# A new hand-written order for a 24-unit kernel: the same operations in another sequence, some on another engine or queue, and fewer warming matmuls

## The chip, the cores and the metric

The kernel runs on one core of a Trainium2 chip. That core has five instruction streams: TensorE (PE in the profile, with its weight loads as PEld), VectorE (DVE), ScalarE (ACT), GpSimd (POOL) and SyncE (SP, which here only starts DMAs). Each stream executes in order, and an instruction that has to wait holds up all that is queued behind it on its own stream. The metric is the device time of one execution in microseconds (us); lower is better. Three executions of the kernel before took 167.09, 168.38 and 167.21 us, median 167.21.

## The reference

Two layers follow one another. The first is a recurrence over time with a decaying state, for 4 batches, 8 heads, 768 steps and 48 channels a head. The second is a two-matrix network with a softmax-weighted activation and a layer norm, over 3072 tokens, 384 model channels and 1024 hidden channels.

```python
for t in range(S):
    cur = einsum('bhd,bhe->bhde', u * k[t], v[t])
    y[t] = einsum('bhd,bhde->bhe', r[t], state + cur)
    state = w[t][..., None] * state + einsum('bhd,bhe->bhde', k[t], v[t])
x = y.transpose(0, 2, 1, 3).reshape(B * S, H * D)
h = x @ w_in
sm = exp(h - max(h)) / sum(exp(h - max(h)))
solu = h * sm
ln = (solu - mean(solu)) / sqrt(var(solu) + 1e-6) * g_ln
out = ln @ w_out
```

## The kernel before

**Units.** The 768 steps are cut into 6 chunks of 128, and with 4 batches this makes 24 units of 128 tokens with all 8 heads; unit i is chunk i // 4 of batch i % 4. A unit needs four inputs of 192 KB each (w, k, r, v). Within a chunk the recurrence becomes matrix work: cumulative sums of log w by two triangular matmuls (`cum`), exponentials of both (`ex`, ScalarE), k and r scaled by them (`kp`, VectorE), transposes of both (`krk`, `krr`) and one copy out of PSUM (`kr`), 8 score matmuls of 64 channels (`M`), a masked copy of the scores (`m`, by VectorE with the mask in the same instruction, or by ScalarE with `sel`, a mask by GpSimd, behind it), and the attention matmuls (`Y`). The bonus term with u is made on the side: p = k * r, q = p * u (GpSimd), its sum `dg` (VectorE), dv = v * dg (GpSimd). It is added to y by VectorE in `y`, or, where ScalarE copies y, by an identity matmul at the head of `Y` ("i" in place of "n"). `vb` rounds v to bf16. The state of a batch goes from chunk to chunk by `S` (matmuls), `et` (ScalarE) and `st` (VectorE).

**The second layer of a unit.** `X` transposes y and `xT` copies it out; `H` is 24 matmuls with w_in; `e` = exp (ScalarE), `he` = h * e (VectorE), `hq` = he squared (VectorE or ScalarE); `Oa` and `Ob` are 12 matmuls each (4 of 385 columns with w_out, 8 of one column for the sums). `sq`, `qm` and `lv` make the row's scale, `o` applies it (ScalarE or VectorE), `out` stores 192 KB. w_out is prepared once: multiplied by g (`gw`, 8 parts), its column mean taken by 8 matmuls into PSUM (`mn`), and the mean added to all 8 parts (`ce`, VectorE). `Oa` of unit 0 cannot start before the last `ce`. w_in is rounded by `wi` (3 parts). Unit 23's second layer is done in halves (`Ha`, `Hb` and their like). Units 20 to 23 get two of their transposes by DMA (`KD`, `XD`, on SyncE's queue).

**What sets the order.** Everything is one list of words, ORDER (lines 21 to 69). A word names a stage, a unit (or a part), and behind the dot an engine, a queue or a PSUM slot: "d", "a", "p" are VectorE, ScalarE and GpSimd; for loads and stores "s" or nothing, "a", "p" are the queues of SyncE, ScalarE and GpSimd; "b0", "s3" and their like are PSUM slots. The loop at lines 563 to 566 emits the stages in that sequence, and the class InOrder (line 74) ties every instruction to the one before it on its engine, so that the list is the program order of every stream. Nothing reorders it afterwards. (All of these instructions are recorded at line 88, the line inside InOrder, so the profile is read by tiles and not by lines.)

```python
    for word in ORDER.split():
        word, _, how = word.partition(".")
        name = word.rstrip("0123456789")
        stages[name](int(word[len(name):]), how)
```

**Rings.** Input tiles are rings of 7 units (NIO), the bf16 v and log w rings of 10, kp/kr/dv rings of 6, the rest 4. [...] `hot` runs are matmuls of 512 columns on a zero tile whose result nobody reads.

**The squares.** Line 470 holds the stage that the prediction turns on; on VectorE both operands are the same bf16 tile in SBUF:

```python
    def hidden_square(i, x, part=ALL):
        he, hq = he_t[i % NWK][:, part], hq_t[i % NWK][:, part]
        if x == "a":
            act.activation(out=hq, in_=he, func=SQUARE)
        else:
            (dve if x == "d" else pool).tensor_mul(out=hq, in0=he, in1=he)
```

Of the kernel before, what the change touches and what calls it, by code (L numbers as in the profile page):

```python
# [30 lines left out]
dv4 ce0 vb5.a krk6.s3 LK8.s H3.b1 et4 ce5 p5 e2 ce6 LR8.s ce2 p6 LV7.a krr6 ce4 Y4.is1 lw7 he2 e3 q5 LW9.s
Oa0.s2 vb6.p hq1.a LK9.s he3 M5.b0 q6 Ob0 y4.a LR9.s LV8.p m5.a kr6.d cum7.b1 Oa1.s1 hq2.d ex7 LW10.s sel5 st4
X4.s3 sq0 M6.b0 lw8 kp7 LK10.s Ob1 xT4.a p7 m6.a qm0 dg5 krk7.s0 LR10.s cum8.b1 hq3.d lv0 krr7 S5.s3 sq1 q7 dg6
ex8 LW11.s H4.b0 qm1 kr7.d o0.a dv5 kp8 LK11.s lv1 Oa2.s2 out0.p e4 o1.d LR11.s dv6 Y5.ns0 dg7 lw9 krk8.s1 y5.d
vb7.p et5 M7.b1 LW12.s Ob2 he4 sel6 m7.a LK12.s X5.s0 lw10 krr8 p8 st5 cum9.b1 vb8.a cum10.b0 xT5.d LR12.s sq2
ex9 kr8.d Oa3.s3 q8 ex10 kp9 LW13.s S6.s0 dv7 Ob3 hq4.a qm2 kp10 LV9.s p9 M8.b1 sq3 et6 lv2 krk9.s1 qm3 st6
H5.b0 p10 LK13.s lw11 m8.d lv3 p11 o2.a LR13.s krr9 dg8 e5 Y6.is0 q9 kr9.d LW14.s cum11.b1 krk10.s2 y6.a he5
S7.s1 out1.p ex11 LV10.s Oa4.s0 q10 lw12 kp11 o3.a krr10 out2 cum12.b0 sel7 et7 X6.s3 st7 ex12 M9.b1 kr10.d
LK14.s Ob4 q11 m9.a xT6.d kp12 krk11.s1 LR14.s out3.p Y7.ns2 lw13 M10.b1 sq4 y7.d vb9.p S8.s3 m10.a LW15.s dg9
dv8 krk12.s2 cum13.b0 LK15.s dg10 krr11 LV11.p ex13 qm4 H6.b1 hq5.d LR15.s kr11.d lv4 sel9 et8 o4.a kp13 krr12  # L40
Y8.ns1 LW16.s e6 p12 Oa5.s0 y8.d st8 kr12.a LK16.s X7.s1 p13 M11.b0 xT7.d S9.s3 dg11 lw14 LR16.s vb10.p Ob5 he6
m11.a dv9 S10.s2 et9 LW17.s LV12.p hq6.d cum14.b1 et10 sq5 H7.b0 ex14 qm5 st9 LK17.s q12 st10 lv5 kp14 krk13.s1
sel10 LR17.s e7 Y9.ns3 krr13 y9.d X8.s2 M12.b1 p14 o5.a LV14.s he7 Oa6.s3 kr13.a dv10 LW18.s krk14.s0 m12.d lw15
Ob6 LV13.p xT8.a LK18.s lw16 cum15.b0 hq7.d sq6 M13.b1 ex15 krr14 q13 qm6 LR18.s m13.d Y10.ns1 lv6 Oa7.s2 sel11
LV15.a kp15 kr14.a H8.b1 vb11.p o6.d dv11 y10.d cum16.b0 e8 LW19.s dg12 X9.s3 q14 Ob7 xT9.d ex16 he8 LK19.s
out4.p X10.s1 krk15.s0 Y11.ns3 sq7 xT10.a vb12.p krr15 LV16.s kp16 p15 M14.b1 kr15.a S11.s1 y11.d out5 H9.b0
vb13.p et11 m14.a qm7 st11 p16 dg13 LR19.s lv7 krk16.s0 hq8.d e9 H10.b1 LW20.s o7.d dv12 vb14.a he9 out6.p krr16
LK20.s e10 X11.s3 Oa8.s1 q15 LV17.s dg14 xT11.a kr16.d M15.b0 q16 lw17 Ob8 out7 m15.a he10 sel14 S12.s2 LR20.s
sq8 lw18 Y12.ns3 hq9.a dv13 Y13.ns0 y12.d cum17.b0 LW21.s H11.b1 hq10.d et12 ex17 vb15.p st12 LK21.s p17 qm8
y13.d LR21.s S13.s3 e11 kp17 Oa9.s2 dv14 lw19 dg15 X12.s0 q17 cum18.b0 et13 lv8 st13 Ob9 xT12.a he11 p18 o8.a  # L50
X13.s3 Y14.ns0 sq9 vb16.a out8 Oa10.s1 q18 ex18 y14.d LW22.s qm9 xT13.d LV18.s lv9 cum19.b1 p19 dg16 S14.s0
LK22.s ex19 kp18 krk17.s3 Ob10 dv15 kp19 LR22.s sel15 M16.b0 sq10 hq11.a krr17 m16.d H12.b1 LW23.s q19 et14 o9.a
kr17.d lw20 out9.p X14.s2 H13.b0 e12 dg17 LV19.p xT14.d qm10 he12 Oa11.s3 dv16 e13 krk18.s2 st14 vb17.p cum20.b1
lv10 he13 Ob11 dv17 ex20 p20 Y15.ns0 o10.a dg18 H14.b0 hq12.a kp20 q20 lw21 y15.d KD20 krk19.s1 LV20.p sq11 e14
krr18 qm11 Y16.ns0 kr18.d M17.b1 out10.p krr19 y16.d LK23.s m17.a S15.s2 hq13.d LV21.s Oa12.s0 lv11 kr19.d p21
vb18.a M18.b1 he14 et15 X15.s1 o11.a sel17 Ob12 vb19.a dg19 m18.a cum21.b0 q21 xT15.d S16.s3 st15 sq12 X16.s1
ex21 out11.p H15.b1 qm12 xT16.a p22 kp21 et16 lv12 S17.s2 e15 hq14.d KD21 Y17.ns1 H16.b0 st16 sel18 vb20.a he15
et17 lw22 LR23.s dv18 o12.a Oa13.s3 dg20 e16 LV22.p y17.d M19.b1 Ob13 he16 m19.a q22 X17.s1 Oa14.s0 sq13 out12.p
xT17.a qm13 hq15.d lv13 cum22.b0 dv19 o13.d H17.b1 ex22 dg21 out13.p dg22 sel19 Ob14 kp22 e17 Oa15.s1 st17 p23
KD22 lw23 he17 hq16.a Y18.ns3 q23 cum23.b0 Y19.ns2 y18.d ex23 M20.b1 dv20 y19.d Oa16.s3 sq14 m20.a kp23 vb21.p  # L60
X18.s2 vb22.p Ob15 qm14 xT18.d KD23 lv14 dv21 X19.s2 sq15 M21.b0 hq17.d H18.b1 m21.a LV23.s xT19.d sel20 o14.d
qm15 lv15 out14.p Ob16 e18 dv22 S18.s2 o15.a Oa17.s0 he18 sel21 sq16 out15 Y20.ns1 M22.b0 hq18.d M23.b1 m22.a
Ob17 y20.d qm16 m23.d XD20 lv16 Y21.ns1 sel22 H19.b0 o16.a dg23 sq17 et18 vb23.p y21.d dv23 S19.s3 st18 e19 XD21
Oa18.s1 et19 he19 Y22.ns2 Ob18 y22.d H20.b1 sq18 qm17 qm18 XD22 st19 lv17 hq19.d Y23.ns2 e20 H21.b0 out16 y23.d
lv18 XD23 he20 Oa19.s3 e21 hq20.d H22.b1 he21 Ob19 e22 o17.d Ha23.b0 out17 sq19 he22 Oa20.s2 ea23 o18.a qm19
Hb23 hq22.d hq21.a out18 Ob20 Oa21.s0 sq20 lv19 qm20 hea23 o19.a Oa22.s1 eb23 out19.p Ob21 lv20 heb23 hqa23.a
Ob22 hqb23.d sq21 qm21 o20.d lv21 Sa23.s3 sq22 out20.p qm22 o21.d Sb23 lv22 Mal23.s2 sq23 o22.a out21.p Mar23.s0
qm23 Mbl23 lv23 out22 Mbr23 ol23.a or23.d outl23.a outr23
"""

NIO, NLW, NKP, NWK = 7, 10, 6, 4
# [525 lines left out]
```

## Time and profile before

| | |
|---|---|
| median of three executions | 167.21 us |
| the profiled execution: time, span | 167.09 us, 165.4 us |
| mean granted clock of TensorE | 0.948 |
| PE busy | 138.8 us (84%) |
| DVE busy | 139.3 us (84%) |
| ACT busy | 119.3 us (72%) |
| POOL busy | 113.5 us (69%) |
| DMA moved | 28.51 MB, mean 172 GB/s |
| start of `mn` on PE; start of `Oa` of unit 0 | 34.27 us; 46.65 us |

The span runs from the first to the last instruction, and 1.7 us of the time lie outside it. The table of the page that cuts the span in 40 slices gives each engine's busy tenths, one digit for 4.1 us. The view by windows gives the same with numbers, and with the granted clock of TensorE in each window: at 0.50 a matmul takes twice its time while PE counts as busy all the same. A timeline row has start, duration, engine and operands, and in brackets the idle time of the engine ahead of it with what ended that.

### The profile page before, as it was taken

To read this page: it belongs to the slowest core of one execution; us is meant where nothing else is said; L and a number is where in the kernel's file an instruction comes from. 1 tells how busy PE (TensorE), PEld (TensorE's weight loads), DVE (VectorE), ACT (ScalarE), POOL (GpSimd) and SP (SyncE) were. 2 spreads that over 40 slices of the span, in tenths; PEclk is the share of its full clock that TensorE was granted. 3 is DMA by queue.
4 is the path that set the end of the run, shared out by engine and by line. 5 is a ranking of instruction groups with operands and counts; after the bars stand their busy time and mean duration, and the time that the engine had idled before them with its cause. 6 is when DMAs were issued, how large, how long until landed. Compare 5 with 4: busy or idle time off the path is not lost.

```text
span 165.4 us, 5234 instructions
## 1 busy us (share of the span) xinstructions
PE 138.8 (84%) x2128; PEld 108.5 (66%) x2128; DVE 139.3 (84%) x238; ACT 119.3 (72%) x245; POOL 113.5 (69%) x139
## 2 busy tenths in 40 slices
PE   6585548845999999904999999999997999999991
PEld 2133336733978787803686898688886778888771
DVE  7028949599999999999899998999989995979661
ACT  3456288791799899960397798988997798546782
POOL 5057697999009999999893569669999399510030
PEclk9999985898799999995699999999999999999999
DMA  5999999997999907999968619195486156213215
GB/s 114 272 235 307 360 325 304 206 255 160 237 237 175 211 4 184 222 224 228 203 167 163 146 55 188 46 192 153 79 231 149 57 115 156 78 33 90 99 50 190
DMA packets 98665, 28.51 MB, mean 172 GB/s; under 512 B 94953, under 2 KB 96882, under 8 KB 98642
## 3 DMA queue, kind: packets, MB, share of 16 engines
q1 hardware_dynamic: 87040, 19.57, 56.1%
q0 software_dynamic: 2080, 6.75, 11.5%
q10 hardware_dynamic: 9522, 1.87, 5.5%
q8 instruction: 16, 0.26, 0.7%
q14 instruction: 7, 0.06, 0.1%
HBM read 22.03 MB, written 4.72 MB: 162 GB/s over the span
## 4 chain that ended last, share of the span: by engine, by line
PE 53%; DVE 18%; issue 8%; SPq 7%; DMA 6%; ACT 5%; ACTq 0%; DVEq 0%
PE o_ps L88 18%; PE h_ps L88 17%; SPq L88 7%; DMA win_f<-in_moe_w_in_dram 5%; PE y_ps L88 4%; PE s_ps L88 3%; DVE w L88 3%; PE m_ps L88 3%; PE kr_ps L88 3%; DVE kp L88 3%; DVE he L88 3%; PE cum_ps L88 2%; DVE st L88 2%; DVE hq L88 2%; DMA kr_in<-in_r_dram 2%
## 5 line engine op out<-in xcount | busy, mean ns | idle before, releaser
L88 PE MATMUL o_ps<-w,he 128*128 128x385 bf16 (+2 forms) x208 | 47.3, 317 | 0.9 <-DVE st L88 0.8
L88 PE MATMUL h_ps<-xT,win_sb 128*128 128x128 bf16 x576 | 38.6, 226 | 0.4 <-DVE m L88 0.4
L88 PEld LDWEIGHTS <-win_sb 128*128 128x128 bf16 x576 | 35.4, 102 | 1.1 <-issue 0.4
L88 DVE TENSOR_TENSOR he<-h_ps,e 128x1024 bf16<-128x1024 f32 (+1 forms) x25 | 29.4, 1175 | 6.1 <-ACT e L88 5.7
L88 PE MATMUL o_ps<-inv_col,e 128*128 128x1 bf16 x192 | 31.2, 166 | 0.0
L88 DVE TENSOR_TENSOR kp<-cum_ps,kr_in 128x768 bf16<-128x768 f32 x24 | 22.7, 948 | 9.8 <-DMA kr_in<-in_r_dram 7.4
L88 PE MATMUL o_ps<-one_col,hq 128*128 128x1 bf16 x192 | 30.6, 163 | 0.0
L88 ACT ACTIVATE e<-h_ps 128x1024 bf16<-128x1024 f32 (+1 forms) x25 | 24.8, 990 | 7.2 <-PE h_ps L88 6.8
L88 POOL TENSOR_TENSOR p<-kr_in 128x384 bf16<-128x384 f32 x24 | 24.9, 1043 | 5.2 <-DMA kr_in<-in_r_dram 5.2
L88 PEld LDWEIGHTS <-hq 128*128 128x128 bf16 x192 | 18.6, 98 | 13.0 <-issue 1.0
L88 POOL TENSOR_TENSOR q<-p,u_bc 128x384 bf16<-128x384 bf16 x24 | 22.9, 952 | 5.3 <-ACT u_bc L88 1.6
L88 ACT ACTIVATE cum_ps<-cum_ps 128x768 f32<-128x768 f32 x24 | 19.2, 802 | 8.9 <-PE cum_ps L88 4.8
L88 POOL TENSOR_TENSOR dv<-vb,dg 128x384 bf16<-128x384 bf16 x24 | 20.4, 850 | 6.0 <-DVE dg L88 4.2
L88 POOL TENSOR_SCALAR_AFFINE_SELECT m<-m 128x1024 bf16<-128x1024 bf16 x15 | 17.0, 1132 | 10.4 <-ACT m L88 9.9
L88 ACT CAST m<-m_ps 128x1024 bf16<-128x1024 f32 x15 | 15.3, 1017 | 10.8 <-PE m_ps L88 10.4
L88 DVE TENSOR_TENSOR hq<-he 128x1024 bf16<-128x1024 bf16 (+1 forms) x16 | 20.9, 1308 | 0.1
L88 POOL DMA_DIRECT2D out_dram<-o x14 | 8.2, 584 | 18.5 <-ACT o L88 13.9
L88 PEld LDWEIGHTS <-he 128*128 128x128 bf16 x208 | 19.6, 96 | 1.5 <-DVE o L88 0.3
L88 PEld LDWEIGHTS <-kp 128*128 128x128 bf16 x240 | 15.7, 99 | 7.4 <-DVE kp L88 4.8
L88 PEld LDWEIGHTS <-e 128*128 128x128 bf16 x192 | 18.4, 97 | 1.2 <-issue 1.0
L88 PE MATMUL kr_ps<-ident,kp 128*128 128x128 bf16 x160 | 15.7, 226 | 2.8 <-DVE kp L88 2.8
L88 PEld LDWEIGHTS <-kr 64*128 64x128 bf16 (+1 forms) x272 | 10.7, 97 | 10.1 <-issue 7.3
(83 smaller groups left out, 287.7 us busy)
## 6 DMA issues: line engine op xcount, KB each, us to landing
kr_in<-in_k_dram SPq DMA_DIRECT2D x24, 192.0 KB, 4.2
w_in<-in_w_dram SPq DMA_DIRECT2D x22, 192.0 KB, 4.4
kr_in<-in_r_dram SPq DMA_DIRECT2D x22, 192.0 KB, 4.5
out_dram<-o POOLq DMA_DIRECT2D x14, 192.0 KB, 2.6
v_in<-in_v_dram POOLq DMA_DIRECT2D x11, 192.0 KB, 4.5
out_dram<-o SPq DMA_DIRECT2D x9, 192.0 KB, 2.7
v_in<-in_v_dram SPq DMA_DIRECT2D x8, 192.0 KB, 4.8
win_f<-in_moe_w_in_dram POOLq DMA_DIRECT2D x2, 512.0 KB, 5.8
```

What stands on the lines that cost most here:

```text
L88: made = make(*args, **kwargs)
```

## The change

Only ORDER is changed: the functions, the rings and the types stay as they are. Both lists hold the same 24 units of work. These words get another engine or queue (counts of the 24 or fewer words of a kind):

| word | before | after |
|---|---|---|
| `hq` (squares) | 15 VectorE, 8 ScalarE, last unit's halves ScalarE and VectorE | 12 VectorE, 11 ScalarE, both halves VectorE |
| `kr` (copy of transposes) | 12 VectorE, 8 ScalarE | 14 VectorE, 6 ScalarE |
| `xT` | 11 VectorE, 9 ScalarE | 6 VectorE, 14 ScalarE |
| `o` (scaled output) | 8 VectorE, 15 ScalarE | 12 VectorE, 11 ScalarE |
| `vb` | 14 GpSimd, 10 ScalarE | 16 GpSimd, 8 ScalarE |
| `gw` | 4 VectorE, 2 ScalarE, 2 GpSimd | 4 VectorE, 4 ScalarE |
| `wi` | 3 ScalarE | 2 ScalarE, 1 GpSimd |
| loads of v | 11 GpSimd's queue, 8 SyncE's, 5 ScalarE's | 16, 4, 4 |
| loads of w_out (2 halves) | 1 SyncE's, 1 GpSimd's | 2 GpSimd's |
| loads of k; of r | 24 SyncE's; 22 SyncE's and 2 ScalarE's | 23 SyncE's and 1 ScalarE's; 24 SyncE's |
| stores of a whole unit | 14 GpSimd's queue, 9 SyncE's | 7, 16 |
| `hot` matmuls | 17 in 5 runs | 6 in 1 run |

`m` (9 VectorE, 15 ScalarE with `sel` behind them), `y`, `lw`, `LW` and the DMA transposes keep their numbers, though not always their units. In the list the squares on VectorE are those of units 2, 3, 5, 6, 7, 8, 10, 13, 14, 15, 17, 18, 19, 20, 22 before, and 3, 6, 8, 9, 11, 15, 16, 18, 19, 20, 21, 22 after. Ahead of `Oa0` the list has the PE work of `cum` 0 to 6, `krk` and `krr` 0 to 6, `M`, `S`, `Y` 0 to 4, `X` 0 to 3, `H` 0 to 3 before; after, `krk6`, `krr6` and `H3` stand behind `Oa0`, and `X4` ahead of it. Unit 0's loads of r and k stand first on SyncE's queue after, with r of unit 1 next.

```diff
 ORDER = """
-LV0.p pc0 LW0.a LK0.s LW1.a LW2.s hot6.s3 LR0.a LW3.s LU0.a LK1.s lw0 cum0.b0 hot2.s3 LW4.s ex0 lw1 LR1.a
-cum1.b1 hot3.s3 ex1 kp0 p0 LK2.s lw2 ur0 LR2.s krk0.s0 us0.s1 LK3.s cum2.b0 uc0 LV1.a krr0 q0 hot3.s3 LR3.s lw3
-kp1 LV2.a LI0.p ex2 LK4.s p1 dg0 krk1.s2 cum3.b1 vb0.a kr0.d hot3.s3 LR4.s lw4 LI1.p kp2 ex3 dv0 LI2.s LG0.a
-M0.b0 S0.s3 q1 m0.d vb1.a krr1 LW5.s krk2.s1 kr1.a p2 krr2 kp3 et0 LV3.a M1.b0 q2 dg1 kr2.a cum4.b1 krk3.s0 m1.d
-p3 Y0.ns2 krr3 ex4 S1.s1 LO0.s y0.d vb2.p kr3.a LK5.s q3 dg2 S2.s2 st0 wi0.a dv1 kp4 X0.s3 M2.b0 et1 LO1.p xT0.a
-dg3 krk4.s0 wi1.a st1 p4 m2.d Y1.is1 wi2.a LR5.s M3.b1 q4 krr4 gs0.s3 m3.d LW6.s gc0 H0.b0 et2 dv2 vb3.a kr4.d
-y1.a LV4.p lw5 Y2.is3 st2 e0 M4.b1 dg4 dv3 S3.s1 LK6.s y2.a he0 gw3.p Y3.is0 m4.a X1.s2 X2.s3 LR6.s et3 xT1.d
-gw0.a gw1.p cum5.b1 xT2.d H1.b0 st3 y3.a ex5 gw2.d LV5.p gw6.d gw5.a gw4.d gw7.d e1 LW7.s kp5 mn0.s2 he1 LK7.s
-lw6 hq0.a krk5.s3 vb4.p cum6.b1 LV6.p X3.s1 ce1 LR7.s krr5 ex6 H2.b0 ce7 sel4 ce3 kr5.a LW8.s kp6 S4.s0 xT3.a
-dv4 ce0 vb5.a krk6.s3 LK8.s H3.b1 et4 ce5 p5 e2 ce6 LR8.s ce2 p6 LV7.a krr6 ce4 Y4.is1 lw7 he2 e3 q5 LW9.s
-Oa0.s2 vb6.p hq1.a LK9.s he3 M5.b0 q6 Ob0 y4.a LR9.s LV8.p m5.a kr6.d cum7.b1 Oa1.s1 hq2.d ex7 LW10.s sel5 st4
...
-dv8 krk12.s2 cum13.b0 LK15.s dg10 krr11 LV11.p ex13 qm4 H6.b1 hq5.d LR15.s kr11.d lv4 sel9 et8 o4.a kp13 krr12
...
-m11.a dv9 S10.s2 et9 LW17.s LV12.p hq6.d cum14.b1 et10 sq5 H7.b0 ex14 qm5 st9 LK17.s q12 st10 lv5 kp14 krk13.s1
...
-ex21 out11.p H15.b1 qm12 xT16.a p22 kp21 et16 lv12 S17.s2 e15 hq14.d KD21 Y17.ns1 H16.b0 st16 sel18 vb20.a he15
...
-qm23 Mbl23 lv23 out22 Mbr23 ol23.a or23.d outl23.a outr23
+pc0 LK0.s LW0.a LU0.a LR0.s hot6.s3 LW1.a LR1.s LW2.s LV0.p lw0 LK1.a LW3.s cum0.b0 ur0 us0.s0 ex0 LR2.s p0 lw1
+kp0 uc0 LK2.s LV1.a q0 krk0.s1 cum1.b1 LR3.s dg0 krr0 vb0.p ex1 LI0.p kr0.a kp1 dv0 LW4.s lw2 p1 krk1.s2 S0.s3
+LK3.s cum2.b0 M0.b1 q1 ex2 krr1 m0.d LI2.s LI1.p vb1.a lw3 kr1.d p2 LK4.s et0 LG0.a kp2 M1.b1 LV2.a q2 st0
+cum3.b0 wi0.p krk2.s0 dg1 S1.s1 LR4.s m1.d krr2 et1 Y0.is2 ex3 dv1 LW5.s lw4 kr2.d LV3.p y0.a kp3 M2.b1 wi1.a
+X0.s3 LO0.p xT0.d krk3.s0 m2.d cum4.b0 p3 LK5.s wi2.a dg2 LO1.p gs0.s2 LR5.s Y1.ns3 krr3 gc0 ex4 q3 y1.d H0.b1
+st1 vb2.p LV4.s kp4 p4 X1.s3 e0 kr3.d LW6.s dv2 xT1.a he0 M3.b0 krk4.s2 vb3.p m3.a krr4 q4 Y2.is1 kr4.d lw5 sel3
+y2.a dg3 M4.b1 gw0.a S2.s0 m4.d cum5.b0 et2 LK6.s LV5.p gw2.a X2.s3 S3.s2 dg4 et3 H1.b1 ex5 dv3 st2 gw1.a gw3.d
+gw7.d gw6.a Y3.is1 gw4.d e1 gw5.d LR6.s p5 kp5 mn0.s0 y3.a he1 LW7.s vb4.p xT2.a hq0.a krk5.s1 dv4 X3.s3 krr5
+LK7.s ce6 xT3.a LV6.p ce0 lw6 Y4.is3 LR7.s ce4 kr5.a cum6.b0 ce1 H2.b1 ce3 LW8.s LV7.a p6 ce2 y4.a ce7 ex6 LK8.s
+vb5.p S4.s1 ce5 LV8.p X4.s3 e2 kp6 Oa0.s0 LR8.s q5 lw7 st3 H3.b0 hq1.a LW9.s xT4.d q6 he2 et4 vb6.a LK9.s
+krk6.s2 p7 Ob0 e3 dg5 st4 LR9.s cum7.b1 sq0 he3 lw8 krr6 Oa1.s3 ex7 kr6.a LW10.s M5.b0 kp7 p8 Ob1 hq2.a qm0 m5.d
...
+krk12.s2 LV14.p hq6.d m11.a H7.b0 y8.d LR15.s lv5 dv10 st8 o5.d cum13.b1 LW16.s vb12.p krr12 ex13 Oa6.s3 out5
...
+krk14.s0 ex16 H9.b0 st11 dv12 LV17.s qm7 y11.d lw17 p15 kp16 vb14.a LK19.s S12.s1 lv7 krr14 e9 hq8.d out6.p
...
+hq9.d LW21.s X12.s3 krr16 LV19.p sq8 H11.b0 vb16.a qm8 kp17 xT12.a LV20.s kr16.a p17 y13.d LK21.s M15.b1 e11
...
+Ob10 out9.p vb19.a p20 krr18 sq10 cum19.b0 xT14.a qm10 kr18.d S15.s3 ex19 LV21.p H14.b1 hq11.d et15 lv10 kp19
...
+or23.d ol23.a outr23 outl23.a
 """
```

## The prediction

> **What bounds the kernel now.** I read the page's engine shares and its 40 slices first, then the windows around the worst slices, then the timelines of VectorE and GpSimd there, then the waits of PE.
>
> ```profile
> PE 138.8 (84%) x2128; PEld 108.5 (66%) x2128; DVE 139.3 (84%) x238; ACT 119.3 (72%) x245; POOL 113.5 (69%) x139
> ...
> PE   6585548845999999904999999999997999999991
> DVE  7028949599999999999899998999989995979661
> POOL 5057697999009999999893569669999399510030
> PEclk9999985898799999995699999999999999999999
> ```
>
> Four engines are nearly full, and PE stands at 9 from slice 11 on with one hole (0 and 4 in slices 18 and 19). So the end is set by how early PE's stream fills up, and by holes after that. By windows, PE is busy 30.00 of the 30 us from 40 to 70 and 68.39 of the 70 us from 85 to 155. Between them lies the hole:
>
> ```profile
> 70.00:75.00 5.00, 0.61 (x11) 0.49 (x9) 5.00 (x1) 2.94 (x6) 4.98 (x7) 0.94 1.03 222
> 75.00:80.00 5.00, 3.21 (x39) 2.12 (x39) 4.18 (x7) 0.00 (x0) 4.98 (x6) 0.50 0.98 208
> 80.00:85.00 5.00, 5.00 (x83) 4.07 (x83) 4.86 (x8) 3.42 (x8) 4.45 (x6) 0.87 0.94 199
> ```
>
> Columns: window, length, busy time (instructions) of PE, PEld, DVE, ACT, POOL, PE's clock, DMA. DVE is "busy" for 5.00 us with one instruction, and PE then runs at half clock. At full clock PE did 0.61*0.94 = 0.57, 3.21*0.50 = 1.60 and 5*0.87 = 4.35 us of work in 15 us: the hole costs 15 - 6.5 = **8.5 us**. The timelines name the instruction and its neighbours on GpSimd:
>
> ```profile
> 68.95 7.18 DVE L88 TENSOR_TENSOR hq<-he 128x1024 bf16<-128x1024 bf16 x1
> 76.06 0.68 DVE L88 COPY kr<-kr_ps 128x1024 bf16<-128x1024 bf16 x1
> ...
> 70.50 1.95 POOL L88 TENSOR_TENSOR p<-kr_in 128x384 bf16<-128x384 f32 x2
> 72.40 0.49 POOL L88 CAST vb<-v_in 128x384 bf16<-128x384 f32 x1
> 72.86 0.82 POOL L88 TENSOR_TENSOR dv<-vb,dg 128x384 bf16<-128x384 bf16 x1
> 73.64 0.94 POOL L88 DMA_DIRECT2D v_in<-in_v_dram  x1
> 74.60 0.92 POOL L88 TENSOR_TENSOR q<-p,u_bc 128x384 bf16<-128x384 bf16 x1
> 75.47 1.61 POOL L88 TENSOR_SCALAR_AFFINE_SELECT m<-m 128x1024 bf16<-128x1024 bf16 x1
> ```
>
> This is `hq5.d`. The same instruction takes 0.68 us where GpSimd is idle (129.77, 148.00); here it ends 7.18 us after its start, while GpSimd runs eight instructions without a gap, and the next mask takes 1.61 in place of some 1.1. Other squares on VectorE beside a busy GpSimd took 1.34, 1.40, 1.24 and 2.43 us (81.42, 87.50, 101.88, 123.70). The two engines shut each other out. Copies from PSUM (`kr`, 0.68 throughout) never show it. All longer squares add up to 10.3 us over 15 instructions.
>
> [...]
>
> **Part 1: engines.** Sums by mean rows. VectorE: three squares fewer (3*0.68 = -2.0), a half square more (+0.42), `kr` +2*0.68, `xT` -5*0.35, `o` +4*0.61: +0.4 us. ScalarE: `hq` +3*1.06 - 0.61, `kr` -2*1.01, `xT` +5*0.48, `o` -4*0.58, `vb` -2*0.50, `gw` +2*0.64, `wi` -1.07: -0.1. GpSimd: v loads +5*0.94, a w_out load +0.82, `vb` +2*0.55, `gw` -2*1.25, stores -7*0.58, and `wi` on GpSimd, which no row shows: between 0.55 (a cast of 384 columns) and 2.5 (two of `gw`); I take 1.4, near the cast scaled by columns. Together +1.5. No engine gets lighter; PE's work is the same but for 11 warming matmuls, which fill idle time in the first 15 us. So a gain or loss comes from sequence alone.
>
> **Part 2: the head, up to `Oa0` (46.65 us before).** Three rows show what waits there now:
>
> ```profile
> 12.69 0.96 DVE L88 TENSOR_TENSOR kp<-cum_ps,kr_in 128x768 bf16<-128x768 f32 x1 [3.11 <-DMA kr_in<-in_r_dram]
> ...
> 21.11 1.01 ACT L88 COPY kr<-kr_ps 128x1024 bf16<-128x1024 bf16 x1 [3.34 <-DMA win_f<-in_moe_w_in_dram]
> ...
> PE mean_ps L88 <- DVE w L88: 3.3, 2, 3.0
> ```
>
> The loads of r for units 0 and 1 move to second and third place on SyncE's queue, so the waits of 4.31 and 3.11 us ahead of `kp0` and `kp1` shrink. ScalarE no longer issues `LV3`, whose issue at 20.69 held everything behind it (3.34 us). Against that, both halves of w_out now stand on GpSimd behind `wi0`, which waits for w_in. By rows: `q0` ends near 10.5, then `vb0` and the load of w_in (18 with 5.8 us to landing), `wi0` to 19.5, `dv1`, `LV3`, then the two loads at about 22 and 23.7, landing 5.7 to 9.6 us later: 28 to 33. Before, they landed by 24.6 and 29.1, and VectorE began `gw` only at 33.44. So w_out is just in time, and from there VectorE has four `gw` (5.58 us before, also beside a GpSimd without gaps), `kp5`, `he1` and eight `ce` of 0.48: 5.6 + 0.9 + 1.1 + 3.9 = 11.5, plus about 1 for `mn`: `Oa0` at 33 + 12.5 = 45.5. Bounds: 42 (VectorE's list up to there sums to 25.7 by rows against 26.4; start 7.4, 4 us of waits for GpSimd, 5 of idle) and 50 (w_out lands at 37, the 9.6 us load behind one that delays it). I take 45.5, -1.1. But PE then still owes `H3`, `krk6` and `krr6`, less `X4`: 1.34 + 0.22 + 0.22 - 0.19 = **+1.6**. The head is worth +0.5 us.
>
> Fewer warming matmuls: PE's clock is 0.82 and 0.50 in 20 to 30 us though 17 ran before. The six that are left end near 4 us. If the clock is halved in 5 to 20 us, PE there has some 5 us of work in 15, so it would cost at most 5 us and, with idle time on both sides, probably nothing; I take 0 and keep the 5 in the range.
>
> [...]
>
> **Part 3: the hole.** `hq5` goes to ScalarE, so -8.5 us. What is late next: squares on VectorE in the stretch where GpSimd is full are now 3, 6, 8, 9, 11, 15, 16, 18, 19. Of the squares above, the four short waits were hidden or nearly so (0.6 to 0.7), and 1.75 at 123.70 cost PE 0.97 in 125 to 130. With nine such meetings, each GpSimd boundary having been won by VectorE in about half the cases, one wait of four or five GpSimd instructions is about even odds. I take +4 us; bounds 0 and 17 (two holes like today's).
>
> **Part 4: loads and the tail.** Seven stores move to SyncE's queue, where each waits for its `o` and holds the loads behind it. A load stands 6 to 18 us of VectorE's work ahead of its use in the new list, and only one such wait shows now (86.03, 2.81 us, with 0.2 us of PE idle in 85 to 90): 0, at most 3. The tail after 155 has the same halves: 0.
>
> **The sum.** 167.1 (the profiled execution, span 165.4 and 1.7 around it; 0.1 below the median) + 0.5 - 8.5 + 4 = 163.1; since both halves of the head's estimate lean early, I give **162.5 us**.
>
> **Rivals.**
> - Clean: no new hole and `Oa0` at 43: 167.1 - 8.5 - 3.6 + 1.6 = 156.6. For it: GpSimd's longest idle time before (8.28 us up to 49.42, behind a mask that waited for ScalarE's `m4`) made the backlog that `hq5` met; the new list has `sel3` early and the next only at unit 7. Against: `gw` still meets a full GpSimd.
> - The hole moves: one square waits as `hq5` did: 162.5 - 4 + 8.5 = 167.0, no change.
> - Slower: GpSimd runs further ahead of VectorE in the new list. Adding rows along it, GpSimd has 88.5 us of work ahead of `hq11.d` against VectorE's 83.6 (4.9 more; at `hq5.d` before it was 2.0), so it may be full there while 8, 9 and 11 are squared. Two waits of seven instructions: 158.5 + 2*8.5 = 175.5; a hole and a half, 171. It decides from 10.3 us of such holes on, which gives 168.8. Against: before, a lead of 4.4 at `hq18.d` did no harm, as GpSimd was idle then.
>
> **How the numbers follow.** Forecast (158.5 to 165.5) 0.48, clean 0.11, the same 0.12, slower 0.29. One per cent is 1.7 us, about what a measurement of this kernel can tell from no change. Faster 0.59, within 0.12, slower 0.29. The range 156 to 171.5 takes in clean and a hole and a half, and leaves about 0.05 below and 0.13 above.
>
> **What will show it.** Right: no VectorE square above 3 us, PE at 9 from about slice 11 to the tail, `Oa0` between 44 and 47 us, no ScalarE wait on a w_in landing before 25 us. Wrong: `w_out` landing after 35 us with PE idle ahead of `mn`; a clock of 0.5 in the first 20 us with `H0` later than 27.5; a square of several us on VectorE with PE at 0 and the clock at 0.5 behind it; VectorE waiting for k or r behind a store.

## The result, and the profile after

The changed kernel takes 156.73 us, the median of four executions (155.79 to 158.43), against 167.34 us for the kernel before on the same chip (four, 167.09 to 168.38). The ratio is **0.9336**, with a 95% interval of 0.9272 to 0.9401: 6.6% faster. The forecast of 162.5 us had the direction, and the range from 156 to 171.5 just holds the median, but the gain forecast was 4.7 us and the one measured 10.6. Ratios here and below compare undisturbed executions; for two of the experiments too few were left for an interval.

The profiled execution took 156.87 us with a span of 155.2 us, 10.2 us less than the one before. These are the lines of its page that answer to those shown of before (shares of the span, then the 40 slices, 3.9 us each):

```profile
PE 135.5 (87%) x2117; PEld 107.0 (69%) x2117; DVE 134.1 (86%) x237; ACT 118.8 (77%) x245; POOL 112.9 (73%) x139
...
PE   6365967789999999999995939998999999999991
...
DVE  7337989899999999999999998699999797488681
...
POOL 5399889869568699999999971988389965640100
PEclk9955696599999999999999995999999999999999
```

PE stands at 9 from slice 10 on (35 us; from slice 11, 41 us, before). The hole of slices 18 and 19 is gone, and there are two shallower ones, in slices 22 and 24. By windows (length, busy time and instructions of PE, PEld, DVE, ACT and POOL, PE's clock, DMA share, GB/s):

```profile
80.00:85.00 5.00, 3.28 (x63) 2.84 (x60) 5.00 (x4) 3.04 (x5) 4.98 (x7) 1.00 0.95 203
85.00:90.00 5.00, 4.40 (x70) 3.35 (x64) 5.00 (x6) 4.53 (x8) 4.98 (x6) 1.00 1.11 270
90.00:95.00 5.00, 3.04 (x35) 1.96 (x36) 4.97 (x7) 1.62 (x6) 2.18 (x3) 0.80 0.71 137
95.00:100.00 5.00, 5.00 (x83) 4.24 (x82) 3.23 (x8) 4.22 (x10) 3.72 (x5) 0.86 0.53 121
```

At a clock of 0.50 the 24 matmuls of an `H` took 2.74 us (27.47 of the kernel before), at 1.00 they took 1.50 (82.56). Counted at full clock, PE lost 1.72 + 0.60 + (5 - 3.04*0.80 = 2.57) + (5 - 5*0.86 = 0.70) us there, and 0.65 more at 105.8: **6.2 us** of holes, against 8.5 + 1.55 = 10.05 before. VectorE's timeline has the two squares behind them, `hq8` and `hq9`, and GpSimd's has their neighbours:

```profile
79.70 3.16 DVE L88 TENSOR_TENSOR hq<-he 128x1024 bf16<-128x1024 bf16 x1
...
87.56 3.40 DVE L88 TENSOR_TENSOR hq<-he 128x1024 bf16<-128x1024 bf16 x1
```

```profile
87.64 1.10 POOL L88 TENSOR_SCALAR_AFFINE_SELECT m<-m 128x1024 bf16<-128x1024 bf16 x1
88.69 0.91 POOL L88 TENSOR_TENSOR q<-p,u_bc 128x384 bf16<-128x384 bf16 x1
89.56 0.82 POOL L88 TENSOR_TENSOR dv<-vb,dg 128x384 bf16<-128x384 bf16 x1
90.35 1.38 POOL L88 TENSOR_TENSOR q<-p,u_bc 128x384 bf16<-128x384 bf16 x1
```

`hq9` came 0.08 us ahead of a mask and got in at 87.56 + 3.40 - 0.68 = 90.28 (0.68 being its time alone), as the third instruction from there ended. All longer squares on VectorE together took 7.7 us more than 0.68 each (10.3 before). The forecast's worst case did not come, but its kind of wait did, at two of the three squares that it named.

The larger part of the gain is in the head. PE's timeline shows when `H` of unit 0, `mn` and `Oa` of unit 0 start:

```profile
20.59 1.50 PE L88 MATMUL h_ps<-xT,win_sb 128*128 128x128 bf16 x24 [0.21 <-DVE m L88]
...
32.15 1.48 PE L88 MATMUL mean_ps<-w,mean_w 128*128 128x384 bf16 x8
...
38.03 0.32 PE L88 MATMUL o_ps<-w,he 128*128 128x385 bf16 x1
```

These were 27.5, 34.27 and 46.65 us before. VectorE's timeline up to `Oa0`, where the kernel before spent 5.58 us in four parts of `gw`:

```profile
29.44 2.38 DVE L88 TENSOR_SCALAR w<-wout_f,gr 128x384 bf16<-128x384 f32 x4
31.74 0.94 DVE L88 TENSOR_TENSOR kp<-cum_ps,kr_in 128x768 bf16<-128x768 f32 x1
33.04 1.22 DVE L88 TENSOR_TENSOR he<-h_ps,e 128x1024 bf16<-128x1024 f32 x1 [0.35 <-ACT e L88]
34.18 3.79 DVE L88 TENSOR_TENSOR w<-w,mean_ps 128x384 bf16<-128x384 bf16 x8
```

`gw` starts at 29.4 (33.44 before) and takes 2.38 us; the eight `ce` run in one piece and end at 37.97, and `Oa0` follows at once. So the 10.2 us are: head 46.65 - 38.03 = 8.6, less the 1.6 us of work that PE still owes there (the prediction's estimate), is **-7.0**; holes 6.2 - 10.05 = **-3.8**; a rest of +0.6 is not accounted for.

The last `ce` is not the only thing that `Oa0` needs, though. The same head was traced three times more (runs 4, 11 and 16 below). There `gw` started at 28.3 to 28.8, `mn` at 29.4 to 30.4, and the last `ce` ended at 36.4 to 38.0, yet `Oa0` came at 37.98 to 38.52 all the same. In these three PE stood idle for 1.07, 2.50 and 1.62 us at `X4`, which is ahead of `Oa0` in the list, until ScalarE had copied `y4`; and `y4` started right behind ScalarE's issue of the load `LV7`, at 37.3 to 37.7. So in the new head two chains end within 2 us of each other, and an earlier `ce` alone would not bring `Oa0` below some 38 us.

### The profile page after: what moved, and what is told of

It reads as the page before. It is cut to its first block, busy times and chain, and to the rows that moved or that the text cites. A ratio compares the mean times of both kernels' runs of the same rounds, so it can differ in the third digit from the quotient of the medians.

```text
span 155.2 us, 5210 instructions
## 1 busy us (share of the span) xinstructions
PE 135.5 (87%) x2117; PEld 107.0 (69%) x2117; DVE 134.1 (86%) x237; ACT 118.8 (77%) x245; POOL 112.9 (73%) x139
## 3 DMA queue, kind: packets, MB, share of 16 engines
q10 hardware_dynamic: 7442, 1.48, 4.6%
## 4 chain that ended last, share of the span: by engine, by line
PE 52%; SPq 17%; DVE 16%; issue 5%; DMA 3%; ACT 2%; POOL 2%; DVEq 0%; ACTq 0%; POOLq 0%
PE o_ps L88 21%; SPq L88 17%; PE h_ps L88 14%; DVE kp L88 4%; PE m_ps L88 3%; PE y_ps L88 3%; DVE hq L88 3%; PE s_ps L88 3%; DMA kr_in<-in_r_dram 3%; PE cum_ps L88 3%; PE kr_ps L88 3%; DVE he L88 2%; PE x_ps L88 1%; DVE y L88 1%; DVE st L88 1%
## 5 line engine op out<-in xcount | busy, mean ns | idle before, releaser
L88 PE MATMUL h_ps<-xT,win_sb 128*128 128x128 bf16 x576 | 37.1, 222 | 0.3 <-DVE m L88 0.2
L88 PEld LDWEIGHTS <-win_sb 128*128 128x128 bf16 x576 | 34.0, 100 | 0.7 <-ACT gr L88 0.3
L88 DVE TENSOR_TENSOR he<-h_ps,e 128x1024 bf16<-128x1024 f32 (+1 forms) x25 | 29.4, 1175 | 5.0 <-ACT e L88 4.9
L88 POOL TENSOR_TENSOR q<-p,u_bc 128x384 bf16<-128x384 bf16 x24 | 22.2, 933 | 1.8 <-ACT u_bc L88 1.1
L88 PEld LDWEIGHTS <-kp 128*128 128x128 bf16 x240 | 16.4, 103 | 6.9 <-DVE kp L88 3.6
L88 POOL TENSOR_SCALAR_AFFINE_SELECT m<-m 128x1024 bf16<-128x1024 bf16 x15 | 16.4, 1096 | 6.3 <-ACT m L88 6.3
L88 PE MATMUL kr_ps<-ident,kp 128*128 128x128 bf16 x160 | 16.3, 232 | 3.1 <-DVE kp L88 3.1
L88 DVE TENSOR_TENSOR hq<-he 128x1024 bf16<-128x1024 bf16 (+1 forms) x14 | 16.6, 1189 | 0.0
L88 ACT ACTIVATE lw<-w_in 128x384 bf16<-128x384 f32 x24 | 12.3, 521 | 4.3 <-DMA w_in<-in_w_dram 4.2
```

The costliest lines, as they stand in the source:

```text
L88: made = make(*args, **kwargs)
```

## The experiments

Each edit is to ORDER alone, except in the two with tests of their own.

**1. The hole by itself.** Before, with one word changed:

```diff
-... H6.b1 hq5.d LR15.s kr11.d ...
+... H6.b1 hq5.a LR15.s kr11.d ...
```

> The list of before with one letter changed: the square of unit 5 on ScalarE instead of VectorE. Theory 'hole' (the 7.18 us square that waits for GpSimd costs PE 8.5 us, and nothing takes its place): 167.3 - 8.5 + about 0.5 for ScalarE's extra 1.06 us, so 158 to 161, PE full through 70 to 85 us, clock 1.0 there. Rival 'backlog' (GpSimd is full from 50 to 80 us, so the next squares on VectorE, of units 6 and 7, wait as long instead): a square of 3 us or more at 75 to 90 us and 163 to 168. In both Oa of unit 0 stays at 46.6.

Measured: 161.46 us, ratio 0.9544 (0.9477 to 0.9612), just above the 158 to 161 expected, and no square of 3 us or more. The windows of this run where the kernel before had PE at 0.61, 3.21 and 5.00, with half the clock in the middle:

```profile
70.00:75.00 5.00, 4.28 (x78) 3.26 (x76) 3.72 (x7) 4.72 (x10) 4.98 (x7) 1.00 0.90 189
75.00:80.00 5.00, 3.85 (x67) 3.25 (x66) 5.00 (x7) 3.93 (x9) 4.98 (x6) 1.00 1.05 219
```

GpSimd is as full as it was (4.98), and of the hole 0.72 + 1.15 us of idle PE are left in these ten. `hq6`, next in line, takes 2.19 us instead of 1.34. The hole was worth 7.6 us net.

**2 and 3. The head of one list with the rest of the other.** The words ahead of `Oa0` were put in the other list's order, on its engines and queues: the changed head before the old rest, then the old head before the changed rest. No work is added or left out.

> The words ahead of Oa0 in the list of before, in the sequence and on the engines of after (6 warming matmuls, unit 3's scores masked by GpSimd and unit 4's not); behind Oa0 the list of before, hq5 on VectorE as there. Theory 'head' (the head is worth some 7 us by itself): Oa0 at 38 to 40 and 158 to 161 us if the hole stays, about 150 to 153 if the hole goes with GpSimd's backlog. Rival 'head is only moved forward' (VectorE or GpSimd are the bound behind it and give the gain back): Oa0 at 38 to 40 but 164 or more.

> The words ahead of Oa0 in the list of after, in the sequence and on the engines of before (17 warming matmuls); behind Oa0 the list of after. Theory 'head': Oa0 at 44 to 47 and 156.7 + 6 to 8, so 163 to 165. Rival 'hole alone': 156 to 158, as the tail of the list is what made the gain.

Measured: 0.9777 (0.9714 to 0.9839; six executions, 165.19 to 168.61 us) and 0.9985 (0.9927 to 1.0042; ten, 167.50 to 176.16). The profiled executions took 168.61 and 170.67 us. In the first, `H0` came at 21.36 and `mn` at 29.37 (20.59 and 32.15 in the changed kernel), but `Oa0` only at 44.78. PE's timeline says why:

```profile
39.68 2.14 PE L86 MATMUL h_ps<-xT,win_sb 128*128 128x128 bf16 x24 [3.94 <-DVE kp L86]
41.61 1.06 PE L86 MATMUL kr_ps<-ident,kp 128*128 128x128 bf16 x8
44.78 0.48 PE L86 MATMUL o_ps<-w,he 128*128 128x385 bf16 x1 [2.12 <-DVE kr L86]
```

`H3` and `krk6` stand ahead of `Oa0` in the old list's set and wait for VectorE. In the second, the same seam cost two waits of 4.92 and 2.51 us, `Oa0` came at 54.05, and all behind it was the changed kernel shifted, `hq8` at 3.16 and `hq9` at 3.40 us again. A head must fit the words that follow it; neither half alone shows what it is worth. The expectations of both theories were missed, for `Oa0` and for the time.

**4. The warming matmuls.** The changed kernel with the 11 `hot` matmuls put back.

```diff
-... cum0.b0 ur0 ... cum1.b1 LR3.s ... krr0 vb0.p ... krk1.s2 S0.s3
+... cum0.b0 hot2.s3 ur0 ... cum1.b1 hot3.s3 LR3.s ... krr0 hot3.s3 vb0.p ... krk1.s2 hot3.s3 S0.s3
```

> The list of after with the 11 warming matmuls of before put back behind cum0, cum1, krr0 and krk1. Theory 'clock' (the clock of 0.77, 0.50, 0.71 in 5 to 20 us delays the head): clock 1.0 up to 20 us, Oa0 1 to 3 us earlier, 154 to 155.5. Rival 'the head waits for loads and for the other engines': Oa0 within 0.7 us, 156 to 157.5, or later if the matmuls hold PE up.

Measured: 157.01 us, ratio 0.9274 (0.9201 to 0.9347), no difference from 0.9336 that could be told. The clock is 1.00 in all six windows of the first 30 us, where the changed kernel has 1.00, 0.77, 0.50, 0.71, 0.98 and 0.50, and `Oa0` comes at 38.4 instead of 38.0. Half the clock on a PE that waits for the other engines anyway (busy for 2.10, 3.39, 4.50, 2.97 and 3.94 us of each five from 5 to 30) cost nothing that shows here.

**5 to 8. What made the head early.** Three parts of the change, made in the kernel before one at a time and together:

```diff
-LV0.p pc0 LW0.a LK0.s ... LR0.a ... LR1.a ... et0 LV3.a ... gw2.d LV5.p gw6.d gw5.a gw4.d gw7.d ...
+LV0.p pc0 LW0.a LK0.s LR0.s LR1.s ... et0 LV3.p ... gw2.a LV5.p gw6.a gw5.a gw4.a gw7.a ...
```

> The list of before with the load of v for unit 3 on GpSimd's queue instead of ScalarE's, as after has it. Theory 'ScalarE's wait' (its 3.34 us behind that issue delays w_in's casts and H0): H0 at 24 to 25.5 instead of 27.5, Oa0 at 44 to 45.5, 165 to 166.5. Rival 'VectorE's list sets Oa0': H0 earlier, but gw on VectorE within 0.7 us of 33.4 and Oa0 within 0.7 us of 46.6.

> The list of before with the four parts of gw that VectorE makes (2, 4, 6, 7) on ScalarE. Theory 'exclusion in the head' (these four take 5.58 us because GpSimd shuts VectorE out; on ScalarE, next to PSUM reads, they take 0.64 each): mn ends 2 to 3.5 us earlier than 39.4, Oa0 at 43 to 44.5, 163.5 to 166. Rival 'ScalarE is the bound there': mn no earlier than 38.5 and 166.5 to 168.5.

> The list of before with the loads of r for units 0 and 1 right behind k of unit 0 on SyncE's queue. Theory 'first loads': kp0 at 6.3 and kp1 at 9 to 10 instead of 8.35 and 12.69, Oa0 1 to 3 us earlier, 164 to 166.5. Rival 'slack' (VectorE has idle time in the head anyway): the same kp0 and kp1, Oa0 within 0.7 us of 46.6, 166.5 to 168.

> The list of before with three changes: v of unit 3 loaded from GpSimd's queue, gw 2, 4, 6, 7 on ScalarE, and the loads of r for units 0 and 1 right behind k of unit 0 on SyncE's queue. If the head's 8.6 us come from waits that can be taken one by one: kp0 at 6.3, kp1 at 9 to 10, Oa0 at 39 to 41.5, 161 to 164 with hq5's wait still there. Rival 'the order of the PE list' (krk6, krr6 and H3 stand ahead of Oa0 and wait for kp6): Oa0 not before 42.5, 164 to 167.

Measured:

| edit | ratio (95%) | `H0` | `mn` | `Oa0` |
|---|---|---|---|---|
| none (before) | 1 | 27.47 | 34.27 | 46.65 |
| v of unit 3 on GpSimd's queue | 165.25 us (160.90 to 166.77), no interval | 25.98 | 32.29 | 44.78 |
| `gw` on ScalarE | 0.9824 (0.9756 to 0.9891) | 27.96 | 34.76 | 44.05 |
| r of units 0 and 1 first | 1.0057 (1.0020 to 1.0094) | 26.41 | 33.42 | 46.48 |
| all three | 0.9713 (0.9639 to 0.9788) | 25.35 | 31.89 | 41.18 |

The load of v (run 5) brings `gw` on VectorE 2.0 us forward, to 31.45, and `Oa0` by 1.9, as its theory expected; of its four executions one took 160.90 us and three 165.15 to 166.77, and what parts them was not traced. `gw` off a VectorE that meets a full GpSimd (busy for 5.57 of those 5.58 us before) gives 1.8% by itself (run 6). The early r (run 7) brings `kp0` to 6.65 and `kp1` to 10.12 (8.35 and 12.69 before) and yet gives nothing: `kp3` then waits 1.93 us for its own r, `gw` starts only 0.85 us earlier, at 32.59, and takes 6.16 us instead of 5.58. The three together (run 8) move `Oa0` by 5.5 us, and the time by 4.8, while `hq5` stays at 7.20 us.

**9. Three parts and the hole.** The same with `hq5.a`.

> The list of before with four changes taken together: v of unit 3 loaded from GpSimd's queue, gw 2, 4, 6, 7 on ScalarE, r of units 0 and 1 loaded first on SyncE's queue, and hq5 on ScalarE. Theory 'two places' (the head, worth 4.9 us in the run without hq5, and the hole, worth 7.5 us alone, are independent): 167.2 - 4.9 - 7.5 = 154.8, so 153.5 to 156.5, level with after. Rival 'shared backlog' (an earlier head only lets the next square on VectorE wait): 158 to 162.

Measured: 0.9291 (0.9210 to 0.9372). The two shares, 2.9% and 4.6%, add up to 7.5%, and 7.1% is measured: head and hole are nearly independent. Eight words changed in the old list bring it level with the whole new list.

**10. The rest of the head.** The run above still has `Oa0` at 40.66. On top of it, `H3`, `e3`, `krk6` and `krr6` were put behind `Oa0`:

```diff
-... krk6.s3 LK8.s H3.b1 et4 ... krr6 ce4 ... e3 q5 LW9.s Oa0.s2 vb6.p hq1.a LK9.s he3 M5.b0 q6 ...
+... LK8.s et4 ... ce4 ... q5 LW9.s Oa0.s2 H3.b1 vb6.p hq1.a e3 LK9.s he3 M5.b0 krk6.s3 krr6 q6 ...
```

> The kernel before with four edits of the list: v of unit 3 loaded on GpSimd's queue, four parts of gw from VectorE and GpSimd to ScalarE, r of units 0 and 1 loaded first, hq5 on ScalarE; and now also H3, krk6 and krr6 (and e3 with them) behind Oa0, as in the changed kernel. Theory 'PE's own order': what still parts this head from the changed kernel's is the PE work that stands ahead of Oa0; so Oa0 comes at 38 to 39.5 us (40.7 without this edit) and the time is 154 to 155.5 us. Rival 'VectorE's ce sets Oa0': the last ce ends when it did, Oa0 stays within 0.7 us of 40.7 and the time at 155.5 to 157.

Measured: 0.9522 (0.9415 to 0.9629; five executions, 158.84 to 166.43 us), slower than without the edit, and the numbers of both theories are missed. The profiled execution was the longest, 166.43 us: `mn` came 2.3 us later in it and `Oa0` at 42.91, and `hq8` met a full GpSimd for 5.21 us, with 2.96 us of idle PE behind it. Whether that holds for the shorter ones is not shown, so why the edit costs time stays open. But from `mn` to `Oa0` it took 9.27 us, against 9.28 without the edit, and now PE stood idle for 1.76 us ahead of `Oa0`, waiting for the last `ce`: PE's order does not set `Oa0` there. VectorE's timeline of run 9 has what does set it:

```profile
34.79 1.23 DVE L86 TENSOR_TENSOR he<-h_ps,e 128x1024 bf16<-128x1024 f32 x1 [2.49 <-ACT e L86]
35.93 1.48 DVE L86 TENSOR_TENSOR w<-w,mean_ps 128x384 bf16<-128x384 bf16 x3
37.32 0.95 DVE L86 TENSOR_TENSOR kp<-cum_ps,kr_in 128x768 bf16<-128x768 f32 x1
38.19 2.40 DVE L86 TENSOR_TENSOR w<-w,mean_ps 128x384 bf16<-128x384 bf16 x5
```

A wait of 2.49 us for ScalarE's `e1` ahead of `he1` (0.35 in the changed kernel), and `kp6` between the `ce` (0.9; behind `Oa0` in the changed kernel): 2.14 + 0.9 = 3.0 of the 3.4 us between the 9.28 and the changed kernel's 5.88, in these two executions. (In the three other traces of the changed head `mn` to `Oa0` takes 7.6 to 9.2 us, because of the wait at `X4` told above.)

**11. The holes that are left.** The changed kernel with its two long squares on ScalarE:

```diff
-... e9 hq8.d out6.p ... ex17 hq9.d LW21.s ...
+... e9 hq8.a out6.p ... ex17 hq9.a LW21.s ...
```

> The list of after with the squares of units 8 and 9 on ScalarE; on VectorE they took 3.16 and 3.40 us, and PE lost 5.6 us between 80 and 100 us. Theory 'hole' as for unit 5 of before (where 7.5 us of 8.5 came back): 156.7 - 3 to 5, so 151.5 to 154. Rival 'the wait moves on' to units 6 or 11, or ScalarE becomes late (2.1 us more): 155 to 158.

Measured: **152.4 us, ratio 0.9104** (0.9040 to 0.9169), within the 151.5 to 154 expected: by the ratios 2.5% below the changed kernel, and the fastest of all. The same four windows:

```profile
80.00:85.00 5.00, 4.96 (x93) 4.36 (x91) 3.72 (x6) 4.97 (x10) 4.98 (x8) 1.00 1.06 226
85.00:90.00 5.00, 4.42 (x72) 3.46 (x70) 3.96 (x7) 4.93 (x9) 4.98 (x6) 1.00 1.05 242
90.00:95.00 5.00, 5.00 (x92) 4.17 (x89) 4.97 (x9) 4.90 (x12) 3.63 (x6) 1.00 0.95 193
95.00:100.00 5.00, 5.00 (x84) 4.17 (x82) 4.64 (x8) 4.91 (x12) 4.98 (x7) 1.00 0.62 157
```

ScalarE goes from 13.41 to 19.71 us busy in these 20, nearly full, and PE from 15.72 (at a lower clock) to 19.38.

**12. GpSimd's idle time.** Before, GpSimd idles for 8.28 us up to 49.42, and the prediction held that this made the backlog that `hq5` met. Here the mask of unit 5 is taken from it (`m5.d`, no `sel5`).

> The list of before with unit 5's scores masked by VectorE in its copy, so that GpSimd has no mask to wait for there; GpSimd stood idle for 8.28 us ahead of that mask. hq5 stays on VectorE. Theory 'backlog' (hq5 waits because GpSimd then runs late and without a gap): GpSimd idle less than 4 us before 50 us, hq5 under 4 us, PE's hole under 3 us, 159 to 163 in spite of 1.1 us more for VectorE. Rival 'place in the list' (GpSimd is full there anyway): hq5 6 us or more and 166 to 169.

Measured: 169.57 us (four executions, 166.83 to 172.05), no interval. GpSimd idles for 9.88 us all the same, now ahead of `dv`, and `hq5` takes 8.05 us. So the edit did not take the idle time away and does not test the theory by itself. Runs 6 and 8 do: there GpSimd idles for only 5.29 and 5.06 us ahead of that mask, and `hq5` takes 7.18 and 7.20 us, as with 8.28 before. How long GpSimd idles there does not set the wait. (The mask that it waited for was that of `m5`, not of `m4` as the prediction had it.)

**13. The exclusion in isolation.** Behind the last store of the changed kernel, three VectorE instructions of a kind, first with GpSimd idle and then beside a run of GpSimd instructions without waits:

> The list of after, with a row of small tests behind its last store (time and total are not compared): three VectorE instructions of one form each, with GpSimd idle, and beside ten GpSimd instructions that have nothing to wait for (products of 384 columns, masks of 1024, casts of 384, a mixture). Theory 'exclusion': with GpSimd idle 0.68 for a square, about 0.3 to 0.5 for a part of gw, 1.2 for a product out of PSUM; beside GpSimd the squares and gw wait for one or more whole GpSimd instructions, the product out of PSUM not at all. If a wait ended with the GpSimd instruction that is running, the three squares would take 0.7 to 1.8 us each; if a run of GpSimd instructions without a gap holds them off, the first would take 5 us or more. Rival 'inputs were late, not the port': all forms take the same beside GpSimd as alone.

VectorE's timeline. First three squares, three parts of `gw`, three products from PSUM and three copies alone; then squares beside GpSimd's products and beside its masks; then `gw`, PSUM products and copies beside GpSimd's products (squares beside casts and a mixture took 2.70 and 3.71):

```profile
150.29 1.89 DVE L98 TENSOR_TENSOR hq<-he 128x1024 bf16<-128x1024 bf16 x3
152.27 1.07 DVE L98 TENSOR_SCALAR w<-wout_f,gr 128x384 bf16<-128x384 f32 x3
153.42 3.48 DVE L98 TENSOR_TENSOR hq<-h_ps,e 128x1024 bf16<-128x1024 f32 x3
156.99 1.09 DVE L98 COPY hq<-he 128x1024 bf16<-128x1024 bf16 x3
...
159.71 3.94 DVE L98 TENSOR_TENSOR hq<-he 128x1024 bf16<-128x1024 bf16 x3
169.74 4.47 DVE L98 TENSOR_TENSOR hq<-he 128x1024 bf16<-128x1024 bf16 x3
...
197.44 2.95 DVE L98 TENSOR_SCALAR w<-wout_f,gr 128x384 bf16<-128x384 f32 x3
206.46 3.48 DVE L98 TENSOR_TENSOR hq<-h_ps,e 128x1024 bf16<-128x1024 f32 x3
215.15 3.14 DVE L98 COPY hq<-he 128x1024 bf16<-128x1024 bf16 x3
```

The squares, the parts of `gw` and the copies, which read SBUF alone, are held up (1.89 to 3.94, 1.07 to 2.95, 1.09 to 3.14); the PSUM product is not (3.48 and 3.48). Not all that reads SBUF alone is: the sum `dg` took 0.53 to 0.55 us in all 24 places of the kernel before. A square beside products takes some 0.7 us more and one beside masks some 0.9, less than such a product (0.90) or mask (1.08) takes alone, so each waits for one GpSimd instruction at most. That does not explain 7.18 us.

**14. GpSimd's own sequence in isolation.** The same place, with the string of GpSimd instructions that stood beside `hq5`.

> The changed kernel with nine tests behind its last store, so that its time is not the kernel's. In each test GpSimd runs a string of instructions without waits (s mask, p product of fp32 inputs, q product, v product with a broadcast, c cast, d a DMA load that it issues), and VectorE runs two squares beside it; in the tests named he the square's input is made by VectorE out of PSUM right ahead of it. The strings sppcvq and dsppcvdqsp are the sequence that stood beside hq5 before. Theory 'kinds': masks or fp32 products keep VectorE out over several instructions; a square takes 3 us or more beside pppppppp or dssssss in one row and at most 2 beside vvvvvvvv and dqqqqqq. Theory 'issue': a DMA issue inside the string does it; squares are above 3 us in the strings with d alone. Rival 'alignment': nothing in the sequence does it, the square waits for one GpSimd instruction each time (0.7 to 2.3 us) in all nine tests, and the wait over seven instructions stays unexplained.

VectorE's timeline, first the first square of the test with the string *sppcvqspp* and squares behind their own input, then both squares of the test with the same string and no such input:

```profile
174.27 6.26 DVE L117 TENSOR_TENSOR hq<-he 128x1024 bf16<-128x1024 bf16 x1
...
183.72 2.88 DVE L117 TENSOR_TENSOR hq<-he 128x1024 bf16<-128x1024 bf16 x2
```

The square waits through seven instructions, with neither a DMA issue nor a wait in the string; met at another moment, the same string costs two squares 2.88 us together. Beside eight fp32 products two squares took 2.80 us, and beside six masks behind a DMA issue 6.59 us (0.72 and 5.95). So long waits need no special kernel around them. 'Issue' fails, as the string with 6.26 us holds no DMA issue, and so does 'alignment' with its one instruction in all nine tests. 'Kinds' has its numbers (above 3 us beside the masks, 1.23 to 1.40 for each square beside `v` and `q` products), but masks do not do it by themselves: in run 13 three squares beside masks took 1.48 to 1.57 us each, and the wait of 6.26 us went through products and a cast as well.

**15 and 16. The moment or the list.** `hq5` of before behind the next `kr`, and `hq9` of the changed kernel behind `qm8` and `kp17`, both still on VectorE:

```diff
-... hq5.d LR15.s kr11.d ...
+... LR15.s kr11.d hq5.d ...
```

> The kernel before with hq5, still on VectorE, moved behind the next copy kr of unit 11, so that it comes to its turn some 0.6 us later (by the rows of before 69.55 us, 0.11 us after the start of GpSimd's mask sel9, where it came 0.49 us ahead of it, during a DMA issue). GpSimd's list beside it is the same. Theory 'moment': how many of GpSimd's instructions a square waits for depends on the moment at which it comes; hq5 now waits for one or two (2.6 us at most in all), PE's hole shrinks and the time is 160 to 162.5 us. Rival 'list': GpSimd full for 8 us shuts the square out wherever it comes; hq5 takes 6 us or more and the time is 166 to 168.

> The changed kernel with hq9, still on VectorE, moved behind qm8 and kp17, so that it comes some 0.9 us later, at about 88.4 us and 0.78 us into GpSimd's mask sel14 (it came 0.07 us ahead of that mask and waited for it and two more). Theory 'moment': hq9 waits for one instruction, 0.4 to 1.6 us in all its 0.68, and the time is 154.5 to 156. Rival 'list': hq9 takes 2.5 us or more and the time stays at 156 to 157.5.

Measured: 1.0013 (0.9971 to 1.0056) and 0.9278 (0.9196 to 0.9359). For `hq5` the rival 'list' holds. VectorE, then GpSimd in that run:

```profile
70.43 6.45 DVE L88 TENSOR_TENSOR hq<-he 128x1024 bf16<-128x1024 bf16 x1
```

```profile
75.34 0.92 POOL L88 TENSOR_TENSOR q<-p,u_bc 128x384 bf16<-128x384 bf16 x1
76.20 1.62 POOL L88 TENSOR_SCALAR_AFFINE_SELECT m<-m 128x1024 bf16<-128x1024 bf16 x1
```

`hq5` came 0.75 us later by GpSimd's list (0.26 us into `sel9`, where it had come 0.49 us ahead of it) and got in at the very place where it had got in before: at the end of `q12`, ahead of `sel10` (at 70.43 + 6.45 - 0.68 = 76.20). PE still lost 5.05 us in one wait. `hq9` took 2.25 us instead of 3.40, between the numbers of the two theories. It came 0.02 us into the `q` behind the mask, not inside the mask as intended, waited for two instructions, and got in where it had got in before, between `dv14` and the last `q` of the stretch; it had only come later. The time, 155.37 us, does not tell it from the changed kernel (the intervals overlap).

## Why the prediction was right and wrong

**The hole of `hq5`, -8.5: right.** One word gave 7.6 us (run 1); 1.9 us of smaller waits of PE stand in the same ten. That GpSimd's idle time ahead of 49.42 made the wait, which the prediction used in favour of the clean case, does not hold: the wait is the same with 5.06 us of it (run 12).

**The new waits, +4: right in size, wrong in the picture.** The changed kernel's holes are 6.2 us against 1.55 left of before, so +4.7, and of the 5.6 us of them between 80 and 100 us only 0.6 is left once `hq8` and `hq9`, two of the squares named, are on ScalarE (run 11). But the odds per boundary, "won by VectorE in about half the cases", were a poor model: `hq5` took 7.18 to 8.14 us in all seven runs that kept it on VectorE in its place (6.45 when moved), `hq14` 2.42 or 2.43 in ten of eleven runs with the old list there, `hq9` 3.40 in three. In these runs such a wait mostly came again with the list, but not always: `hq8` of the old list took 0.68 in ten runs and 5.21 in run 10. That the odds came to +4 beside a measured +4.7 is luck. That one wait can hold several GpSimd instructions stood in the timelines of before: there `hq5` waited through seven, from `sel9` at 69.44 to the end of `q12` (it got in at 68.95 + 7.18 - 0.68 = 75.45).

**The head, +0.5: the step that failed.** `Oa0` was put at 45.5, with 42 as the early bound, and came at 38.03. By the prediction's own sum (start of `gw` at 33, then 5.6 + 0.9 + 1.1 + 3.9 and 1 for `mn`) the 7.5 us are three terms in the profiled execution:

- The start of VectorE's `gw`, 29.4 and not 33: 3.6 us. The prediction followed w_out (issue at 22 and 23.7, landing at 28 to 33) and took it for just in time. The issues stand at 17.93 and 19.66 on GpSimd's timeline and landed a median 7.2 us later, so w_out waited for VectorE. VectorE's list ran early, as unit 0 did (`H0` at 20.6, not 27.5). Against the 33.44 of before, the load `LV3` alone gave 2.0 us of this start (run 5) and the r loads alone 0.85 (run 7); the rest was not taken apart. `wi0` on GpSimd took 1.04 us, where 1.4 was taken.
- `gw` itself, 2.38 and not 5.58: 3.2 us. The row of before was used as the price, though most of those 5.58 us were waits: the four take 0.36 us each alone, and three of them 2.95 us instead of 1.07 beside GpSimd (run 13). A price that holds a wait is not a price; run 6 has 2.6 us of `Oa0` from moving `gw` alone.
- `mn`: 0.35 us of wait ahead of `he1` where 1 was taken: 0.7 us.

The moves of `LV3` and r were seen, and were credited in words but not in the sum, since w_out was held to be last. `H3`, `krk6` and `krr6` were counted as 1.6 us that PE owes, which the account above takes over unmeasured; that they hold `Oa0` up where VectorE is late was not seen, and shows where the heads were swapped (run 2), not in run 10.

**Warming matmuls, 0: right** (run 4): the clock falls to 0.50 in the head and costs no time that shows, as PE waits for others there. What lowers the clock is not shown. In the hole of before PE idles for 6.18 us, from 70.61 to 76.79, and the clock is 0.50 from 76 to 80; in the changed head it is 0.50 from 8 to 15 us, though PE's longest wait between 1.66 and 8 us is 1.61 us. **Loads and stores, 0: right**: no wait of VectorE for k or r behind a store shows up. **The tail, 0: right** as far as the traces tell: the span ends 3.4 us behind PE's last matmul in both, and PE idles for 0.25 us ahead of its last twelve in the changed kernel.

**Rivals.** Clean, 156.6 at 0.11, has the number by luck: it had `Oa0` at 43 and no hole, where `Oa0` came 5 us earlier and 6.2 us of holes stayed. The mechanism of the slower case was present at 8 and 9, at 2.5 and 2.7 us of wait each, not 6.5.

## What to carry to other kernels

When a row's mean is used as a price, look first whether it holds a wait: four `gw` of 0.36 us each had cost 5.58 us, and their place in the list, not their number, was the cost. Where ScalarE has room, give it the squares that VectorE would make beside a GpSimd without a gap (two words gave another 2.5% here, and the best kernel of this study); the products out of PSUM, 3.48 us for three with GpSimd idle or busy (run 13), can stay on VectorE. For the start of a pipeline, follow the last engine's list from its first instruction, not one load that looks late.

## What the runs showed of the hardware

A square on VectorE, 0.68 us beside an idle GpSimd, took 6.45 to 8.14 us as `hq5`, in the kernel before through seven GpSimd instructions in a row, and 6.26 in isolation, through seven again (run 14), while others met just as full a GpSimd and waited for one (1.31 to 1.57 us in all, run 13). Neither DMA issues, nor GpSimd's waits, nor one kind of instruction decides it by itself (the string with 6.26 us held neither issue nor wait, and squares beside masks took 1.48 to 1.57 us in one test and 5.95 in another), and coming 0.75 us later into the same list did not change where the wait ended: `hq5` got in ahead of `sel10` in five of the runs and one instruction later, ahead of `p14`, in three (PE's wait behind it was 6.2 us in four of the five and 5.05 in the one with `hq5` moved, and 7.0 or 7.1 in the three). What marks those places was not found; it stays open. The second surprise is how exactly such waits repeated (2.42 or 2.43 us for `hq14` in ten runs). It is no rule: `hq8` of the old list, 0.68 us in ten runs, took 5.21 in an eleventh, so a second profile is worth having.
